# Values split one group ahead in attention, and slot lists read behind w2's low parts

## The chip, the cores and the metric

The program runs on one core of a Trainium2 chip. Its engines are TensorE (PE, with its weight loads shown as PEld), VectorE (DVE), ScalarE (ACT), GpSimd (POOL) and SyncE (SP, which here only issues transfers). The metric is the device time of one execution in microseconds (us); smaller is better.

## The reference

Causal attention for 4 batches of 12 heads, 448 rows of 64 values each, and behind it a mixture of 8 experts in which every token goes to one expert:

```python
scores = scale * np.matmul(q, k.transpose(0, 1, 3, 2))        # (4, 12, 448, 448), masked above the diagonal
attn = np.exp(scores - max) / (sum + 1e-09)
x = np.matmul(attn, v)  ->  (1792, 768)
logits = x @ w_gate + modality_bias[modality_id]
e_idx = np.argmax(logits, axis=1);  gate_w = softmax(logits) at e_idx
out[mask_e] = gate_w[mask_e, None] * (np.maximum(x[mask_e] @ w1[e], 0.0) @ w2[e])   # for each expert e
```

Everything is float32. w1 is 768 x 1024 and w2 is 1024 x 768 for each expert.

## The kernel before

The program is written as one fixed order of instructions for each engine; nothing is rescheduled. An engine stops at an instruction whose inputs or whose buffer are not ready, and all that stands behind it on that engine waits too. Float32 accuracy is had by splitting each number into a high and a low part (names with h and l) and adding products of the parts.

**Attention.** There are 48 heads (4 batches of 12), taken in 12 groups of `GH` = 4 heads. `iteration(n)` runs 48 times and is a pipeline over heads. In iteration n, PE makes the scores of head n (`st_scores`, L277), transposes the weights of head n-2 (`st_trans`, L306 and L313), multiplies the weights of head n-3 with the values (`st_pv`, L338 and L345), and for finished groups combines heads into token rows (`st_comb`, L398). ACT takes exponentials (L294), DVE the row maxima (L284) and low parts (L325), and both empty the products (L363, L369).

POOL feeds this in order. At odd n `split_qk((n + 3) // 2)` splits q and k of two heads (L185, L186, L189), which PE needs from iteration n+3 on; between, SP copies the parts into the stacked tile `st` (`stack_qk`, L197 and L198, at even n). At n % 4 == 1, `split_vh` and `split_vl` (L252, L257) split the values of group n // 4 from `vraw` into the tile `vhl`, which has two buffers. Group a's tile is first read by `st_pv` of head 4a in iteration 4a+3 and last by head 4a+3 in iteration 4a+6. `load_v` (L245, L246) has SP fetch the values of a group into the only `vraw`, at n = 4a, once the split of the group before has read it. POOL also normalises half of the token rows (`st_norm`, L416 and L426, at odd n), and for each of the four batches it scatters four slot lists into DRAM (`scatter`, L509). Near the end it splits w1 (L681, L682).

**Between attention and experts.** The first step of the experts (t = 0) has two blocks of 128 tokens, 0 and 1; all of this is straight code. PE runs the first product of both blocks (`pre_g1`), transposes h (`h_trans`, L793), and runs the second product `g2` (L765 to L767) with w2. w2 is split in 8 pieces, k = 0 to 7: `w2_chunk` has ACT make the high part (L684) and DVE the low part (L685). `g2` of block 0 needs piece k for its step k. For the step t = 1 SP reads the slot lists back (`ids_for(1)`, tile `idq`, L734), and `fetch_x(1)` has DVE merge the four lists into two index tiles (L744, L745, tile `idg`) and POOL gather the tokens' rows into `xg` (L746). `schedule_b` (L641 to L646, DVE), `schedule_c` (L651, one PE product) and `schedule_d` (L658 to L669, DVE) work out which expert comes in which step. `next_x(1)` has PE transpose `xg` (`x_trans`, L755); step 1 begins with `g1_pair`.

Of the kernel before, what the change touches and what calls it, by code (L numbers as in the profile page):

```python
# [21 lines left out]
def attention_moe(  # L22
# [15 lines left out]
    B, HP, _, _, S = qk.shape  # L38
# [6 lines left out]
    K2 = DF // 128  # L45
    GH = 4
    NG = H // GH
# [194 lines left out]
    def load_v(gr):  # L242
        b, u = divmod(gr, NG)
        c = slice(u * GH * D, (u + 1) * GH * D)
        nc.sync.dma_start(out=vraw[:, 0:3, :], in_=v[b, 0:384, c].rearrange("(t p) c -> p t c", p=128))  # L245
        nc.sync.dma_start(out=vraw[0:64, 3, :], in_=v[b, 384:448, c])  # L246
# [3 lines left out]
    def split_vh(gr):  # L250
        t = T([128, NTL, GH, 2, D], F32R, "vhl", 2)
        P.tensor_scalar(out=t[:, :, :, 0], in0=vsrc, scalar1=1.0, scalar2=0.0, op0=ALU.mult, op1=ALU.add)  # L252
        vhl[gr] = t

    def split_vl(gr):
        t = vhl[gr]
        P.tensor_tensor(out=t[:, :, :, 1], in0=vsrc, in1=t[:, :, :, 0].bitcast(F32), op=ALU.subtract)  # L257
# [127 lines left out]
    def st_comb(gr, i, x=None):  # L385
        b, u = divmod(gr, NG)
        q0, n = QT[i]
        if u == 0:
            xrow[b, i] = row()
            if i == 0:  # L390
                lt_all[b] = lts[b % 2]
                P.tensor_scalar(
                    out=lts[b % 2][:, :, H, :], in0=mb[:, b], scalar1=1.0, scalar2=0.0, op0=ALU.mult, op1=ALU.add
                )
        if x is None:
            x = bank("x")
        for j in range(GH // 2):
            nc.tensor.matmul(  # L398
                x[:n, j * 2 * XW:(j + 1) * 2 * XW], lhsT=ots(gr, j)[:, q0:q0 + n],
                rhs=wi[:, u * (GH // 2) + j].rearrange("p a c -> p (a c)"), start=True, stop=True,  # L400
            )
        cx[gr, i] = V, x
# [401 lines left out]
    def of_block(u):  # L804
        return lambda k: (2 * u + k // 4, (k % 4) * BLK)
# [85 lines left out]
    with tc.manual_schedule():  # L891
# [186 lines left out]
        def iteration(n):  # L1078
            if n and n % 2 == 0 and n + 2 < NHEAD:
                stack_qk((n + 2) // 2)  # L1080
            if n and n % GH == 0 and n < NHEAD:
                load_v(n // GH)
            gr, i = divmod(n - 2 * GH, GH)
            comb = 0 <= gr < B * NG
            if 0 <= n - 4 < NHEAD:
                st_out(n - 4)
            if comb:
                st_move(gr, i)
                st_norm(gr, i)
                b, u = divmod(gr, NG)  # L1090
                if u == NG - 1:
                    later(n + 1, lambda i=i: x_store(b, i))
                    if i == NTL - 1:
                        after_batch(b, n)
            run_todo((n,))
            if n in (2, 3):
                st_trans(n - 2)
            if n < NHEAD:
                st_scores(n)
            if n == 0:  # L1100
                subs.extend(first_split(1))
            if n in (1, 2):
                for f in subs[:1] if n == 1 else subs[1:]:
                    f()
            run_todo(n)
            if n == 0:
                split_vh(0)
                split_vl(0)
            if n in (1, 3):
                clear_kz(n // 2)  # L1110
            if n % 2 == 1 and n + 3 < NHEAD:
                split_qk((n + 3) // 2)
            if n % GH == 1 and n > GH:
                st_sums(n // GH - 1, P)
            if n % GH == RECAT and n > GH:
                st_rec(n // GH - 1)
            if n % GH == 1 and n > 1:
                split_vh(n // GH)
                split_vl(n // GH)
            if 0 <= n - 1 < NHEAD:  # L1120
                st_exp(n - 1)
            if 0 <= n - 2 < NHEAD:
                if n > 3:
                    st_trans(n - 2)
                run_todo(-n)
                st_split(n - 2)
            if 0 <= n - 3 < NHEAD:
                st_pv(n - 3)
                st_low(n - 3)
            gr, i = divmod(n - 2 * GH + 1, GH)  # L1130
            if 0 <= gr < B * NG:
                st_comb(gr, i)
            if n % 2 == 0 and n + 6 < NHEAD:
                load_qk((n + 6) // 2)

# [34 lines left out]
        def part2(t, b, at, late, mid, ys):  # L1170
            g2(ys, at, range(2))
            late()
            mid()
            g2(ys, at, range(2, K2))
            y_out(t, b, ys)
# [60 lines left out]
        def w2_chunk(*ks):  # L1236
            split_w(raw20, w2h, w2l, ks)
# [34 lines left out]
        pre_g1(1, (5,))  # L1272
        h_trans(0, hb, 1, pb)
        ids_for(1)
        fetch_x(1)
        ids_for(2)
        w2_chunk(4, 5)
        ys = [bank("ot"), bank("x")]
# [2 lines left out]
        ha, hb = (relu(o, i) for i, o in enumerate(g1b[1]))  # L1281
        h_trans(1, ha, 0, pa)
        w2_chunk(6, 7)
        sd = schedule_b(*sc_)
        g2(ys, of_block(0), range(4, K2))
        y_out(0, 0, ys)
# [9 lines left out]
                prefetch(0, raw2, w2, K2)  # L1296
                new_w1(1)

        part2(0, 1, of_block(1), lambda: None, mid1, two_banks())
        total = reg(sch[0:1, 4:5], mybir.ALL_ENGINES, 1, NSTEP)  # L1300

        def step(t):
# [121 lines left out]
```

## Time and profile before

| | |
|---|---|
| median of three runs | 534.66 us (532.64 to 536.38) |
| the profiled execution | 537.39 us, span of its instructions 535.7 us |
| attention, first scores to last product with values | 6.6 to 230 us of the span |
| attention to experts, straight code | 230 to 277 us |
| steps of the experts | 277 to 535.7 us |
| PE busy over the span | 484.6 us, 90% |

The three runs spread by 0.7%. A stretch of the span is named below by its start and end in us. In a timeline, the bracket at a row's end is how long the engine stood idle ahead of that instruction and what released it. PEclk is the clock that TensorE was granted, as a share of 2.4 GHz: 1.00 is 2.4 GHz and 0.50 is 1.2 GHz; a number between means that both occurred.

### The profile page before, as it was taken

Reading aid. Unit: us, or ns where it says so; the run is one execution under the profiler, and the core shown is the slowest. Engines: PE = TensorE matmul, PEld = TensorE weight load, DVE = VectorE, ACT = ScalarE, POOL = GpSimd, SP = SyncE. Lnnn points to the kernel's source line nnn. Section 1 sums busy time; section 2 is a strip of 40 time slices with the busy share of each in tenths; the row PEclk is TensorE's granted clock in tenths of the full one; section 3 lists DMA queues with packets and bytes.
Section 4 is the critical chain, followed back from the end, with each engine's and each line's share of the span. In section 5 each row is a group of like instructions: output and inputs, shape, how many; then the busy total and the mean of one; then the engine's idle time right before and its main releaser. Section 6 shows DMA issues by size and latency. Waiting matters only on the chain. (4 is left out here: it accounts for less than half of the span.)

```text
span 535.7 us, 10328 instructions
## 1 busy us (share of the span) xinstructions
PE 484.6 (90%) x3331; PEld 452.3 (84%) x3331; DVE 318.3 (59%) x882; ACT 274.0 (51%) x683; POOL 290.1 (54%) x303
## 2 busy tenths in 40 slices
PE   4789999999888979889799999999999999989971
PEld 4678889989777879778699999999999999978751
DVE  6899889999788999688341103652011120394690
ACT  4587889989687778434221213442112111452820
POOL 7997989889987797972120200841101001193581
PEclk9799999999899999899799999999999999999987
DMA  8697599986888489656259400784201001087000
GB/s 207 159 247 179 146 228 271 257 214 182 229 203 210 107 227 287 211 154 98 61 144 397 141 32 1 251 268 118 78 1 51 29 2 65 26 262 266 5 12 6
DMA packets 44137, 80.75 MB, mean 151 GB/s; under 512 B 15646, under 2 KB 27166, under 8 KB 44064
## 3 DMA queue, kind: packets, MB, share of 16 engines
q1 hardware_dynamic: 41024, 68.89, 47.5%
q0 software_dynamic: 3040, 11.03, 6.1%
q8 instruction: 28, 0.46, 0.4%
q14 instruction: 45, 0.37, 0.3%
HBM read 49.01 MB, written 11.89 MB: 114 GB/s over the span
## 5 line engine op out<-in xcount | busy, mean ns | idle before, releaser
L294 ACT ACTIVATE p<-p,nm 128x448 f32<-128x448 f32 x192 | 94.8, 497 | 3.9 <-DVE nm L284 3.9
L746 POOL DMA_INDIRECT xg<-xs,idg x18 | 20.3, 1129 | 136.1 <-DVEq L1334 75.2
L784 DVE SCALAR_TENSOR_TENSOR htl<-g,hth 128x256 fp32r<-128x256 f32 x40 | 16.8, 424 | 109.5 <-ACT hth L783 109.5
L767 PE MATMUL g<-xh,w1l 128*128 128x256 f32 x240 | 67.9, 283 | 0.0
L766 PE MATMUL g<-xl,w1h 128*128 128x256 f32 x240 | 67.9, 283 | 0.0
L765 PE MATMUL g<-xh,w1h 128*128 128x256 f32 x240 | 67.9, 283 | 0.0
L338 PE MATMUL ot<-ph,vhl 128*128 128x448 f32 x192 | 50.8, 305 | 16.0 <-POOL vhl L257 9.5
L306 PE MATMUL pt<-ident,p 128*128 128x128 f32 x432 | 65.2, 279 | 0.0
L325 DVE TENSOR_TENSOR pl<-pt,ph 128x1024 fp32r<-128x1024 f32 x48 | 58.3, 1216 | 10.8 <-ACT ph L324 10.5
L189 POOL TENSOR_TENSOR kz<-raw,hl 64x448 fp32r<-64x448 f32 x44 | 51.6, 1172 | 6.3 <-DMA table<-ent,si 2.6
L324 ACT ACTIVATE ph<-pt 128x1024 fp32r<-128x1024 f32 x48 | 48.9, 1020 | 11.1 <-PE pt L306 10.8
L306 PEld LDWEIGHTS pt<-ident,p 128*128 128x128 f32 x432 | 54.0, 151 | 0.7 <-issue 0.3
L338 PEld LDWEIGHTS ot<-ph,vhl 128*128 128x128 f32 x192 | 33.6, 194 | 19.2 <-POOL vhl L257 10.9
L783 ACT ACTIVATE hth<-g 128x256 fp32r<-128x256 f32 x40 | 15.2, 383 | 65.5 <-PE g L767 64.7
L825 POOL DMA_INDIRECT out_dram<-row,idg x14 | 14.8, 1056 | 58.5 <-ACTq L1318 32.2
L766 PEld LDWEIGHTS g<-xl,w1h 128*128 128x128 f32 x240 | 46.1, 192 | 0.0
L767 PEld LDWEIGHTS g<-xh,w1l 128*128 128x128 f32 x240 | 46.1, 192 | 0.0
L765 PEld LDWEIGHTS g<-xh,w1h 128*128 128x128 f32 x240 | 46.1, 192 | 0.0
L277 PE MATMUL sa<-st 128*128 128x448 f32 x96 | 32.6, 340 | 10.8 <-DVE st L229 8.3
L363 ACT ACTIVATE hol<-ot 64x448 f32<-64x448 f32 x48 | 26.0, 542 | 28.0 <-PE ot L338 27.2
L284 DVE CUSTOM_DVE_ANT_0 p<-sa,mask 128x448 f32<-128x448 f32 x96 | 36.3, 413 | 3.2 <-PE sa L277 1.3
L284 DVE CUSTOM_DVE_ANT_0 p<-sb,mask 128x192 f32<-128x192 f32 x96 | 36.3, 412 | 0.3
(337 smaller groups left out, 1408.1 us busy)
## 6 DMA issues: line engine op xcount, KB each, us to landing
st<-hl SPq DMA_DIRECT2D x88, 224.0 KB
raw<-in_moe_w_dram SPq DMA_DIRECT2D x24, 512.0 KB
raw<-in_qk_dram SPq DMA_DIRECT2D x22, 448.0 KB
raw<-in_moe_w_dram SPq DMA_DIRECT2D x20, 384.0 KB
vraw<-in_v_dram SPq DMA_DIRECT2D x12, 384.0 KB
xs<-row SPq DMA_DIRECT2D x12, 384.0 KB
ut<-in_moe_w_dram SPq DMA_DIRECT2D x6, 384.0 KB
raw<-in_qk_dram SPq DMA_DIRECT2D x8, 224.0 KB
```

The costliest lines, as they stand in the source:

```text
L189: P.tensor_tensor(out=kz[m % 2][r, a], in0=x[r, 1], in1=hl[r, 2].bitcast(F32), op=ALU.subtract)
L277: nc.tensor.matmul(outs[i], lhsT=a[:, q0:q0 + n], rhs=z[:, :w], start=(last == 0), stop=(last == 1))
L284: V.tensor_tensor_reduce(out=z, in0=o, in1=m, scale=-scale, scalar=3.0e38, op0=ALU.add, op1=ALU.min, accum_out=nm[:n, i:i + 1],)
L294: A.activation(out=z, in_=z, func=AF.Exp, bias=nm[:n, i:i + 1], scale=-1.0, accum_out=sums[:n, b, i, h:h + 1],)
L306: nc.tensor.transpose(out=o, in_=a, identity=ident)
L324: A.activation(out=ph, in_=t, func=AF.Copy)
L325: V.tensor_tensor(out=pl, in0=t, in1=ph.bitcast(F32), op=ALU.subtract)
L338: nc.tensor.matmul(o[:, q0:S], lhsT=t[:rows, kt, h].rearrange("p a d -> p (a d)"), rhs=ph[:rows, c0:c1], start=(n == 0), stop=(n == 1),)
L363: A.activation(out=t, in_=ov[g][64:128, :S], func=AF.Copy)
L765: nc.tensor.matmul(o, lhsT=ah, rhs=bh, start=first, stop=False)
L766: nc.tensor.matmul(o, lhsT=ah, rhs=bl, start=False, stop=False)
L767: nc.tensor.matmul(o, lhsT=al, rhs=bh, start=False, stop=last)
```

## The change

There are two edits.

The first moves the values one group ahead. `load_v(n // 4 + 1)` now stands at n % 4 == 0 (for group 1 in iteration 0, right behind the split of group 0), and `split_vh` and `split_vl` of group n // 4 + 1 stand at the end of the iterations with n % 4 == 2. The second moves `fetch_x(1)` behind the last two pieces of w2, and `mid1` (with `next_x(1)` and the gather for step 2) from behind two steps of block 1's `g2` to behind five.

```diff
         def iteration(n):
...
-            if n and n % GH == 0 and n < NHEAD:
-                load_v(n // GH)
+            if n and n % GH == 0 and n // GH + 1 < B * NG:
+                load_v(n // GH + 1)
...
             if n == 0:
                 split_vh(0)
                 split_vl(0)
+                load_v(1)
...
-            if n % GH == 1 and n > 1:
-                split_vh(n // GH)
-                split_vl(n // GH)
...
             if 0 <= gr < B * NG:
                 st_comb(gr, i)
+            if n % GH == 2 and n // GH + 1 < B * NG:
+                split_vh(n // GH + 1)
+                split_vl(n // GH + 1)
...
         ids_for(1)
-        fetch_x(1)
         ids_for(2)
...
         w2_chunk(6, 7)
+        fetch_x(1)
         sd = schedule_b(*sc_)
...
-        part2(0, 1, of_block(1), lambda: None, mid1, two_banks())
+        ys = two_banks()
+        g2(ys, of_block(1), range(5))
+        mid1()
+        g2(ys, of_block(1), range(5, K2))
+        y_out(0, 1, ys)
```

On POOL the instructions of the split stay almost where they were: the row `rec` ahead of them and the rows `ltp` and `row` behind are the same. This is POOL's order in iterations 29 to 31, where a scatter stands beside them (`vhl` is the split tile, `table` a slot list):

```order
 L189 TENSOR_TENSOR kz_149<-raw,hl 64x448 x2
 L376 TENSOR_SCALAR rec<-sums 128x16
-L252 TENSOR_SCALAR vhl<-vraw 128x16x64
-L257 TENSOR_TENSOR vhl<-vraw,vhl 128x16x64
 L509 DMA table_70<-ent,si 14592x2
+L252 TENSOR_SCALAR vhl<-vraw 128x16x64
+L257 TENSOR_TENSOR vhl<-vraw,vhl 128x16x64
 L416 TENSOR_TENSOR ltp<-cxt,rec 128x32
 L426 TENSOR_TENSOR row<-cxt,rec 128x256
```

The rows that moved now split the values of group 8 where they split those of group 7, and the scatter goes ahead of them. Their tile's buffer was last read by the head whose `st_pv` stands in the same iteration, so they wait for PE there; before, that read lay three iterations back.

At the start of SP's order, the load of group 1's values goes ahead of the load of q and k for heads 6 and 7 and of the first stacked copies (`st`), and it waits until POOL has split group 0:

```order
 L897 DMA bias_sb<-in_moe_modality_bias_dram 128x16
 L927 DMA wi<-in_moe_w_gate_dram 64x6x8 x2
+L245 DMA vraw<-in_v_dram 128x3x256
+L246 DMA vraw<-in_v_dram 64x256
 L179 DMA raw<-in_qk_dram 128x896
 L197 DMA st<-hl 64x896
```

The load at L179 and the four copies behind it moved back by two rows.

On DVE, between attention and experts, the merge of the slot lists (`idg`) stands behind w2's low parts (`w2l`) and the low part of h (`htl`):

```order
 L796 TENSOR_TENSOR htl_3378<-g,hth_3377 128x512
+L685 TENSOR_TENSOR w2l_3364<-raw_115,w2h_3363 128x768
+L685 TENSOR_TENSOR w2l_3366<-raw_116,w2h_3365 128x768
+L796 TENSOR_TENSOR htl_3380<-sa,hth_3379 128x512
+L685 TENSOR_TENSOR w2l_3368<-raw_3373,w2h_3367 128x768
+L685 TENSOR_TENSOR w2l_3370<-raw_3374,w2h_3369 128x768
 L744 TENSOR_REDUCE idg_0_119<-idq 128x1
 L745 TENSOR_REDUCE idg_0_119<-idq 128x1
 L744 TENSOR_REDUCE idg_1_120<-idq 128x1
 L745 TENSOR_REDUCE idg_1_120<-idq 128x1
-L685 TENSOR_TENSOR w2l_3364<-raw_115,w2h_3363 128x768
```

The five rows with a plus stood behind the merge before; the row with a minus is the first of them.

## Rows read from the trace of the kernel before

**Rows 1.** Stages: us; PE, PEld, DVE, ACT, POOL busy; PEclk; DMA share; GB/s

```profile
59.52:123.53 64.01, 62.21 (x504) 58.62 (x504) 59.10 (x193) 59.09 (x171) 57.40 (x64) 1.00 0.88 224
117.81:203.12 85.31, 75.34 (x575) 69.42 (x576) 76.04 (x244) 67.42 (x192) 72.81 (x77) 0.96 0.77 197
276.90:440.00 163.10, 163.10 (x1183) 162.93 (x1183) 40.35 (x84) 41.60 (x87) 30.02 (x23) 1.00 0.35 120
```

**Rows 2.** Who waited for whom on PE: total us, times, longest

```profile
PE ot L338 <- POOL vhl L257: 9.5, 7, 2.1
PE ot L338 <- DVE ut L369: 6.5, 6, 1.9
```

**Rows 3.** Timeline of PE in attention

```profile
189.54 0.44 PE L277 MATMUL sa<-st 128*128 128x448 f32 x1 [0.69 <-DMA st<-hl]
207.57 0.44 PE L277 MATMUL sa<-st 128*128 128x448 f32 x1 [0.31 <-DMA st<-hl]
216.07 0.56 PE L338 MATMUL ot<-ph,vhl 128*128 128x448 f32 x2 [1.61 <-POOL vhl L257]
```

**Rows 4.** Stretches in which PE's clock was down, columns as in Rows 1

```profile
139.03:142.13 3.10, 3.10 (x12) 2.28 (x12) 1.12 (x2) 1.04 (x3) 2.89 (x5) 0.53 0.73 270
158.72:164.00 5.28, 5.28 (x28) 4.45 (x29) 2.94 (x11) 2.51 (x9) 5.03 (x6) 0.68 0.53 119
216.07:221.00 4.93, 4.92 (x27) 4.40 (x28) 1.97 (x4) 2.51 (x9) 4.85 (x5) 0.67 0.24 71
259.85:265.45 5.60, 5.60 (x17) 5.60 (x18) 4.04 (x10) 0.00 (x0) 1.90 (x2) 0.50 0.51 141
```

**Rows 5.** Timeline of POOL in attention

```profile
86.02 1.05 POOL L252 TENSOR_SCALAR vhl<-vraw 128x1024 fp32r<-128x1024 f32 x1
87.15 2.39 POOL L257 TENSOR_TENSOR vhl<-vraw,vhl 128x1024 fp32r<-128x1024 f32 x1
92.41 2.41 POOL L189 TENSOR_TENSOR kz<-raw,hl 64x448 fp32r<-64x448 f32 x2
...
153.63 1.18 POOL L189 TENSOR_TENSOR kz<-raw,hl 64x448 fp32r<-64x448 f32 x1 [2.19 <-DMA table<-ent,si]
166.76 0.24 POOL L416 TENSOR_TENSOR ltp<-cxt,rec 128x32 f32<-128x32 f32 x1 [2.85 <-issue]
...
200.63 2.41 POOL L189 TENSOR_TENSOR kz<-raw,hl 64x448 fp32r<-64x448 f32 x2
```

**Rows 6.** The start: timelines of POOL, SP and PE

```profile
14.23 2.62 POOL L257 TENSOR_TENSOR vhl<-vraw,vhl 128x1024 fp32r<-128x1024 f32 x1
11.47 0.34 SPq L179 DMA_DIRECT2D raw<-in_qk_dram  x1
23.74 0.57 PE L277 MATMUL sa<-st 128*128 128x448 f32 x1
```

**Rows 7.** The start: two stages, columns as in Rows 1

```profile
17.00:18.00 1.00, 0.00 (x0) 0.00 (x0) 0.97 (x3) 1.00 (x6) 1.00 (x2) 1.00 0.00 0
21.00:26.00 5.00, 5.00 (x24) 4.78 (x23) 4.27 (x16) 2.02 (x8) 4.70 (x6) 0.50 0.96 252
```

**Rows 8.** Timelines of DVE, POOL, ACT and PE between attention and experts

```profile
258.57 0.16 DVE L744 TENSOR_REDUCE idg<-idq 128x1 int32<-128x4 int32 x1 [5.53 <-DMA idq<-table]
258.84 1.82 DVE L685 TENSOR_TENSOR w2l<-raw,w2h 128x768 fp32r<-128x768 f32 x2
261.03 1.03 POOL L746 DMA_INDIRECT xg<-xs,idg  x1 [0.30 <-issue]
256.68 1.56 ACT L684 ACTIVATE w2h<-raw 128x768 fp32r<-128x768 f32 x2
259.85 0.69 PE L766 MATMUL ot<-w2l,hth 128*128 128x384 f32 x1 [3.52 <-DVE w2l L685]
269.34 0.82 PE L755 MATMUL g<-ident,xg 128*128 128x128 f32 x6
```

**Rows 9.** Just after the gathered rows moved: one stage, columns as in Rows 1

```profile
265.00:266.00 1.00, 1.00 (x6) 1.00 (x5) 0.00 (x0) 0.00 (x0) 0.00 (x0) 0.74 0.02 6
```

## The prediction

> **What bounds the kernel now.** I read the stages first, then who waits on PE, then PE's and POOL's timelines around the longest waits. The stages [rows 1] show three regimes. From 276.9 to 440 us PE is busy all the time; whatever starts this stretch earlier ends the program earlier, one for one, since nothing there waits for anything but PE. In the middle of attention (59.52 to 123.53) PE is idle 64.01 - 62.21 = 1.8 us out of 64, and the four others are busy 57 to 59 us: five engines are within 10% of each other, so freeing one gives little. From 117.81 to 203.12 PE is busy only 75.34 of 85.31 us, and POOL 72.81.
>
> The edits aim at two waits. PE waits 9.5 us in seven places for the split of the values [rows 2]; the six waits for `ut` are DVE's and stay. Three of the seven are followed by a stretch at a lower clock [rows 4]: 3.10 us at 0.53 lose 3.10 x 0.47 = 1.5 us against the full clock, 5.28 us at 0.68 lose 1.7, 4.93 us at 0.67 lose 1.6, together 4.8. The other wait lies between attention and experts: DVE stands 5.53 us for the slot lists, w2's low parts are queued behind that, and PE waits 3.52 us for them [rows 8]. The 5.60 us that follow run at half the clock [rows 4], which loses 2.8.
>
> **The first edit: what goes.** If no wait for the values came in place of another, 9.5 + 4.8 = 14.3 us would go. That is the ceiling, for three reasons.
>
> The work on POOL is the same. Each group still costs it 1.05 + 2.39 us for the split [rows 5], in nearly the same place; only PE's need for the result comes four iterations later. So POOL's pace decides as soon as it is slower than PE's. That this happens is seen already: PE waits 0.69 us at 189.54 and 0.31 us at 207.57 for the stacked q and k [rows 3], which come from POOL's `split_qk` through SP. The second of these is the scores of head 46; POOL's work for it ended at 200.63 + 2.41 = 203.04 [rows 5]. Up to there PE cannot come out earlier than POOL does. POOL is idle 85.31 - 72.81 = 12.5 us between 117.81 and 203.12, but most of this is its own: twice 2.19 us and once 0.43 it waits for a scatter to land (one is in rows 5), and each scatter has gaps of some tenths around it. What goes when PE runs earlier is the wait of 2.85 us at 166.76 [rows 5], for a row that PE made late since it had stood and then run slowly from 158.72 on [rows 4]. With a smaller one of this kind I count 3.3 us for this stretch; the bounds are 2 (DVE, busy 76.04 us there, takes the rest) and 6 (POOL's idle time beyond its landings, half of it).
>
> The last wait for the values, 1.61 us at 216.07 [rows 3], and the 1.6 us of low clock behind it go in full. After head 46 PE needs nothing more from `split_qk`, and POOL no longer has a split there: it comes to the w1 pieces earlier than before. Bounds: 1.6 (the clock falls for another reason) and 3.2; I take 3.2.
>
> In the ordinary groups up to 123 us PE has 1.8 us of idle time and 0.9 more ahead of it; I take 2.0 (0.5 to 2.7).
>
> **The first edit: what it adds.** The start gets slower. SP may fetch group 1's values only when POOL has read group 0's, at 14.23 + 2.62 = 16.85 [rows 6]. Behind this in SP's order stand the load of q and k for heads 6 and 7, issued at 11.47 before [rows 6], and the copies for head 4. Values (448 x 256 numbers, 448 KB) and q, k (128 x 896, 448 KB) thus move between some 18.5 us and the copies. The DMA engines are empty at 17 to 18 us and move 252 GB/s at 21 to 26 us [rows 7]: 0.9 MB take 3.6 us, some 2 of which fit ahead of the copies. The scores of head 4, at 23.74 [rows 6], come some 2.0 us later, with 0 to 3.6 as bounds, and I see nothing that gives it back, for PE's next waits there are for DVE.
>
> The Trainium skill, page "DMA: Bandwidth & Descriptors", section "Queues, rings and completion order", speaks against this part: within SP's row of rings each DMA engine takes descriptors in the order in which they were put, so what is queued first goes first. By that the copies wait for all 0.9 MB and the start loses 3.6 us less the empty time, so no other sum; if they shared the engines instead, it could be 0. No run here shows which.
>
> The new wait is POOL's for PE: the split of group a+1 needs the buffer that head 4a-1 reads in the same iteration. Queued behind it on POOL are a normalisation and `split_qk` for head 4a+6. From the end of that product PE has three iterations, some 12 us, to head 4a+6 (16 iterations take 64.01 us [rows 1]). POOL needs 3.5 us for the split and 94.82 - 89.54 = 5.3 us from its end to the end of the next `split_qk` [rows 5], in all 8.8, and the copy must land. That leaves 3.2 us for the copy. I cost this wait at nothing; the cover is those 3.2 us. For head 46 the copy came 207.57 - 203.04 = 4.5 us after POOL's end, beside other transfers, so the cover can be gone.
>
> Sum for attention: -2.0 (start) + 2.0 + 3.3 + 3.2 = 6.5 us.
>
> **The second edit.** DVE makes w2's low parts without standing for the lists: the wait of 3.52 us and the 2.8 us of half clock go, 6.3. Two things come late next. ACT makes the high parts of pieces 6 and 7 from 256.68 to 258.24, and DVE's two low parts (1.82 us [rows 8]) end near 259.3; PE, now without a stop, wants the first of them at some 258.2 and waits 0.3. `schedule_b` then stands behind the merge (the lists were there at 258.57), which makes PE wait some 0.4 in `schedule_c`. So 5.6 us, with bounds 2 and 6.3.
>
> The gather's price is nothing as long as it lands before PE's transposes. It was issued up to 262.06 [rows 8] and its bytes had moved by 265.0, when the engines fall idle [rows 9], 3 us later. DVE merges some 0.7 us later than before, so it lands at 265.7. PE comes to the transposes at 269.34 - 5.6 plus three steps of `g2`. A matmul takes 5.60 / 17 = 0.33 us at half clock [rows 4], 0.165 at full, and a step has six: three steps are 3.0 us. That is 266.7, so 1.0 us is left; without the three steps PE would wait.
>
> **The sum.** 6.5 + 5.6 = 12.1 us. The profiled execution took 537.39 us and would take 525.3; it is 2.7 us over the median of the runs. Taken from the median, 534.66 - 12.1 = 522.6 us.
>
> **The rivals.**
> 1. *POOL takes the place of the waits.* Copies for q and k land as late as the values did, and of attention's gain only the last wait of 1.6 remains, the ordinary groups paying for the start. For it: both waits for copies in rows 3. Against it: only 1.0 us of them in the whole trace. 534.66 - 1.6 - 5.6 = 527.5.
> 2. *POOL has more room than counted.* All of 14.3 goes, less the start: 534.66 - 12.3 - 5.6 = 516.8. Against it: POOL's 72.81 us [rows 1].
> 3. *The slot lists come later against PE than before.* A scatter or a fetch slips by some us beside other transfers, PE stands in `schedule_c` or at the transposes, and the second edit brings 2 us: 526.2. For it: only 1.0 us is left for the gather.
> 4. *Slower: POOL waits for PE and then PE for POOL, in every group.* If the copy takes 4.5 us after POOL's end, as for head 46, and not under 3.2, PE waits 1.3 us at head 4a+6 in each of 10 groups, and the clock falls behind it (1.6 us each): 29 us. 534.66 + 29 - 14.3 - 5.6 = 543.8. Against it: in the ordinary groups no wait for a copy is seen.
>
> **How the numbers follow.** Forecast 0.60, rival 1 0.16, rival 2 0.09, rival 3 0.10, rival 4 0.05. The likeliest gives 522.6. Its own bounds are: start 0 to -3.6, ordinary groups 0.5 to 2.7, middle 2 to 6, last wait 1.6 to 3.2, second edit 2 to 6.3. They will not all fall on one side; half of the distance to each end gives some 516 to 528. Rivals 1 and 3 lie within 528; I set 515.5 to 529, which leaves rival 4 and a part of the others outside. A change of 1% is about what a measurement of this kernel can tell from none. Under 529.3 us lie the forecast, rival 2 and most of 1 and 3: 0.85; within 1%: 0.10; slower: 0.05.
>
> **What the profile after would show.** PE has no wait for `vhl` after the first groups. PE's waits for `st` grow beyond 1.0 us, and they stand where scatters are (160 to 205 us). POOL's 2.85 us ahead of a normalisation are gone, and a wait for PE stands ahead of the split. The scores of head 4 come near 25.7, those of head 46 some 3 us before 207.57. Behind the lists there is no stretch at half clock, and `g1_pair` starts some 12 us earlier than at 276.9. I am wrong if waits for `st` or `kz` with a low clock behind them stand in each group, if PE stands at its transposes of the gathered rows, or if the start loses over 4 us.

## The result and the profile after

The changed kernel took 529.11 us (median of 4 runs, 527.26 to 530.47) beside 534.97 us for the kernel before on the same chip: a ratio of 0.9892, 95% interval 0.9844 to 0.9941. Timed again on another chip (after_again, below) it took 527.46 against 530.94 us: 0.9940, 0.9913 to 0.9966. So it is faster, by 3 to 6 us where 12.1 were forecast, and 529.11 lies just above the range of 515.5 to 529.0. The profiled execution of before that the prediction was made from, 537.39 us, was one of its long ones; a second profile of before (before_again) was of a short one, 530.61 us, on a chip where the others took 530.63 to 537.89 us.

The profiled execution of the changed kernel took 529.8 us, its span 528.1. First who waits on PE (total us, times, longest), the rows of attention over 1 us, to be read against [rows 2]:

```profile
PE sa L277 <- DVE st L229: 8.5, 2, 6.7
PE ot L338 <- DVE ut L369: 5.0, 6, 2.1
PE sa L277 <- DMA st<-hl: 4.8, 5, 2.2
PE sa L277 <- DVE row L426: 2.9, 1, 2.9
PE sa L277 <- DVE kz L232: 2.0, 2, 1.0
PE x L484 <- DVE oh L474: 2.0, 2, 1.4
PE sa L277 <- DVE ut L369: 1.6, 1, 1.6
PE sa L277 <- DVE pl L325: 1.1, 1, 1.1
```

No wait for `vhl` is left. In its place stand waits of the scores (`sa`, line 277): 4.8 us for the copies of q and k, and 2.9, 1.6 and 1.1 us put down to DVE instructions that have nothing to do with the scores. In the second profile of the same kernel the waits at the same heads 14, 36 and 42 (0.72, 2.37 and 1.58 us) stand under the copies, so I read these rows as the copies too: 10.4 us of waits for copies (2.2 of them at head 4; before had 1.0 in all) came where 9.5 us of waits for values went. The two rows of `st` and `kz` from DVE are the first heads, as before. PE's timeline at the places that [rows 3] showed, and where the pair stage begins:

```profile
26.02 0.71 PE L277 MATMUL sa<-st 128*128 128x448 f32 x1 [2.23 <-DMA st<-hl]
66.97 0.44 PE L277 MATMUL sa<-st 128*128 128x448 f32 x1 [1.11 <-DVE pl L325]
158.86 0.56 PE L277 MATMUL sa<-st 128*128 128x448 f32 x1 [2.92 <-DVE row L426]
188.89 0.44 PE L277 MATMUL sa<-st 128*128 128x448 f32 x1 [1.64 <-DVE ut L369]
215.26 0.18 PE L484 MATMUL x<-oh,upper 128*128 128x32 bf16 x1 [1.41 <-DVE oh L474]
251.98 0.60 PE L793 MATMUL sa<-ident,hol 128*128 128x128 f32 x4
267.45 0.28 PE L765 MATMUL g<-xh,w1h 128*128 128x256 f32 x1
```

The stages (columns as in [rows 1]): heads 12 to 28, the middle of attention up to head 45, the low-clock stretch behind the last wait, and the stretch that ran at half clock:

```profile
58.19:123.39 65.20, 62.22 (x505) 58.62 (x504) 60.13 (x194) 59.38 (x171) 59.30 (x68) 1.00 0.88 224
117.60:202.00 84.40, 75.34 (x578) 70.36 (x578) 75.59 (x240) 67.63 (x193) 71.12 (x76) 0.96 0.80 197
215.39:218.99 3.60, 3.60 (x35) 3.18 (x32) 3.60 (x14) 3.40 (x11) 3.52 (x3) 1.00 0.95 320
255.00:262.00 7.00, 7.00 (x41) 6.69 (x42) 4.78 (x24) 1.70 (x3) 3.10 (x3) 1.00 0.46 108
```

Up to head 45 the middle takes 84.40 us where it took 85.31, at head 46 the changed kernel is 0.44 us ahead (207.13 against 207.57 in [rows 3]), and the ordinary groups take longer. Only the last two rows are what was forecast: no low clock, and PE busy all the time where it had stood 3.52 us.

Where heads' scores start, and what comes after attention, in all three profiles without the first edit and three with it (us; "lists" is the time from the hidden tile's transposes, 251.98 above, to the pair stage, 267.45 above):

| profile | head 4 | 9 | 31 | 36 | 42 | 47 | lists | span |
|---|---|---|---|---|---|---|---|---|
| before | 23.74 | 46.74 | 134.64 | 161.17 | 189.54 | 211.45 | 21.36 | 535.7 |
| before_again | 22.43 | 43.93 | 132.25 | 159.60 | 187.53 | 209.03 | 19.44 | 528.8 |
| second_alone | 23.37 | 46.33 | 134.22 | 160.05 | 188.30 | 212.57 | 15.48 | 528.1 |
| after | 26.02 | 46.76 | 134.49 | 158.86 | 188.89 | 210.81 | 15.47 | 528.1 |
| after_again | 25.45 | 45.97 | 134.23 | 158.25 | 187.03 | 209.42 | 15.48 | 526.5 |
| first_alone | 26.09 | 47.51 | 134.72 | 159.16 | 189.82 | 211.69 | 17.11 | 528.9 |

Head 47 starts at 211.0 us on the mean without the first edit and at 210.6 with it, while two profiles of before differ by 2.4 us there: no gain is seen. The last product with the values starts at 229.13, 224.74 and 227.22 us without the edit and at 226.84, 227.08 and 229.31 with it, which is no gain either. PE's next wait is ahead of the positions of the last batch (line 480), which come 10.5 to 10.6 us after that product without the edit and 9.1 to 9.2 us with it: this 1.4 us is the one gain of the first edit that all six profiles show. The lists' stretch takes 15.5 us with the second edit, each time, and 17.1 to 21.4 without it.

### The profile page after: what moved, and what is told of

The parts are those of the page before. It is cut to its first block, busy times and chain, and to the rows that moved or that the text cites. A ratio compares the mean times of both kernels' runs of the same rounds, so it can differ in the third digit from the quotient of the medians.

```text
span 528.1 us, 10324 instructions
## 1 busy us (share of the span) xinstructions
PE 480.4 (91%) x3331; PEld 449.1 (85%) x3331; DVE 316.4 (60%) x882; ACT 273.9 (52%) x683; POOL 289.3 (55%) x303
## 5 line engine op out<-in xcount | busy, mean ns | idle before, releaser
L325 DVE TENSOR_TENSOR pl<-pt,ph 128x1024 fp32r<-128x1024 f32 x48 | 58.3, 1214 | 12.3 <-ACT ph L324 12.1
L277 PEld LDWEIGHTS sa<-st 128*128 128x128 f32 x96 | 16.5, 171 | 24.4 <-DVE ut L369 7.6
```

The costliest lines, as they stand in the source:

```text
L277: nc.tensor.matmul(outs[i], lhsT=a[:, q0:q0 + n], rhs=z[:, :w], start=(last == 0), stop=(last == 1))
L325: V.tensor_tensor(out=pl, in0=t, in1=ph.bitcast(F32), op=ALU.subtract)
```

## The experiments

**The two edits apart, and the place of the early load and split.** *second_alone* is before with only `fetch_x(1)` and `mid1` moved; *first_alone* is before with only the values loaded and split early. These two sets of lines are in the diff of the change. The other two kernels alter the changed one:

```diff
 # v_later
 (at the top of iteration(n), behind stack_qk; the call in iteration 0 goes)
+            if n == 2:
+                load_v(1)
 # split_behind
 (behind split_qk instead of at the end of iteration(n))
-            if n % GH == 2 and n // GH + 1 < B * NG:
+            if n % GH == 3 and n // GH + 1 < B * NG:
                 split_vh(n // GH + 1)
                 split_vl(n // GH + 1)
```

> The kernel before with only the second edit (the gather of block 1 behind w2's last low parts, the transposes behind five hidden tiles of block 1). Theory: most of the 5.9 us that the change gave is this edit, and it works without the first one: 4 to 7 us below the kernel before, with no half clock between 255 and 275 us. Rival (the attention part gave the most): at most 2 us.

> The kernel before with only the first edit (values loaded and split one group ahead). Theory: inside attention POOL and the copies of q and k are late instead of the split, so that head 47's scores come within 1 us of the kernel before's 210.8 to 211.5 us, and all that is left is the low clock behind the last wait, some 1.6 us: 0 to 2.5 us below the kernel before in all. Rival (the waits for the split were worth what the prediction said): 6 us below.

> The changed kernel with the second group's values loaded behind the copies of heads 4 and 5 (iteration 2) instead of in iteration 0. Theory: head 4's scores come back from 26.0 to some 23.7 us, but nothing of it is left at head 9, since two waits for the bank of the outputs (1.3 and 1.9 us in the kernel before) take it: within 1 us of the changed kernel, 528 to 530 us. Rival (the start costs what the prediction took off, 2 us): 527 us or less, with every head from 4 to 47 about 2 us earlier.

> The changed kernel with the early split behind the second q, k split of a group (iteration 4g + 3) instead of ahead of it. Theory (the split that stands ahead of a pair's q, k split makes that pair's copies late): the waits ahead of heads 14 and 42 go, 1 to 2 us of the attention come back, 527 to 528 us. Rival (POOL's total work sets it, wherever the split stands, and other heads wait instead): 529 us as the changed kernel. Rival (the next pair is hit harder, having two iterations alone): 531 us.

Against 531.55 us for before on that chip: second_alone 529.26 us, 0.9945 (0.9918 to 0.9972), which is 1.5 to 4.4 us, between the rival's 2 at most and the 4 to 7 that I expected; first_alone 530.16 us, 0.9970 (0.9949 to 0.9991), 1.6 us, as expected, though its profile shows no gain up to the last product. v_later 531.28 us, 0.9992 (0.9963 to 1.0020), a miss: head 4 starts at 22.67 us, but the load, now queued ahead of the next pair's copies, makes head 6 wait:

```profile
35.89 0.71 PE L277 MATMUL sa<-st 128*128 128x448 f32 x1 [5.61 <-DMA st<-hl]
```

Head 31 starts at 138.79 us, 4.6 us after after_again's, and head 47 at 212.98. So the load costs whichever pair's copies stand behind it in SP's order. split_behind 535.09 us, 1.0065 (1.0038 to 1.0092): its second rival (531 us), and more. Who waits on PE there:

```profile
PE sa L277 <- DMA st<-hl: 17.5, 7, 4.2
PE ot L338 <- DVE ut L369: 2.9, 3, 2.0
```

These waits are ahead of heads 4, 8, 16, 24, 32, 36 and 44, that is nearly all ahead of the pair whose q, k split stands next behind the value split; ahead of heads 14 and 42, where the changed kernel waits, they are 0.2 us or none. The 3.4 us of split move with their place, and the copies behind them are late.

**Smaller steps of POOL and DVE.** All on top of the changed kernel: *after_again* is it unaltered; *split_shared* puts the low part behind the second q, k split and leaves the high part; *scatter_behind* issues the slot scatters behind `split_qk`, where the new `run_todo` stands; *choice_scalar* writes one comparison as four:

```diff
 # scatter_behind
-                later(n + 7 + (2 * i, i // 2, 0)[b], lambda i=i: scatter([i]))
+                later(n + (8.5 + 2 * i, 8.5, 7)[b], lambda i=i: scatter([i]))
+            run_todo(n + 0.5)
 # split_shared (behind split_qk; the call at the end of iteration(n) goes)
+            if n % GH == 3 and n // GH + 1 < B * NG:
+                split_vl(n // GH + 1)
 # choice_scalar
-            V.tensor_tensor(out=oh, in0=eq, in1=wide(m2), op=ALU.is_equal)
+            for t in range(NTL):
+                V.tensor_scalar(out=oh[:, t], in0=eq[:, t], scalar1=m2[:, t:t + 1], scalar2=None, op0=ALU.is_equal)
```

> The changed kernel unaltered, timed beside the three that follow on one chip: it is the line that they are held against. The two edits alone gave ratios of 0.9945 and 0.9970 to the kernel before; if they add up, 0.9915. If the first result stands, 0.989 or less (the edits help each other).

> The changed kernel with the slot scatters of batches 0 and 1 issued on POOL behind the q, k split of an odd iteration, so that each has a whole q, k period to land before the next second kz instruction, which waits for it. Theory (in the middle POOL and the copies behind it set the time): POOL's waits for a scatter's landing (6.9 us in three places) fall to under 2 us, the waits of 2.9 and 1.6 us ahead of the scores of heads 36 and 42 go, and 2 to 4 us come off: ratio to the changed kernel 0.993 to 0.996. Rival (the copies' own landing, on DMA queues that are full, sets it): POOL's waits go and the copies' stay, within 1 us of the changed kernel.

> The changed kernel with the routing's choice (one comparison of two tensors in SBUF, which took 1.81 us and ended with POOL's instruction beside it) written as four comparisons with a scalar per partition. Theory (a DVE instruction with two inputs in SBUF waits until POOL's is done): the four together take under 0.6 us also beside POOL's low part, PE's wait of 1.41 us ahead of the third batch's positions goes, and so do the 0.6 us at 105 us: 1 to 2 us less than the changed kernel. Rival (DVE is late for its own load there): PE waits 1 us or more all the same, no change.

> The changed kernel with the value split's high part (1.05 us) where the change put it and its low part (2.35 us) behind the second q, k split of the group: neither pair of q, k has the whole 3.4 us ahead of it. Theory (what is late is the pair whose split stands behind the value split, by as much as stands ahead of it): waits ahead of heads 14 and 42 shrink by two thirds, those ahead of heads 8, 16, 32, 44 grow by less than the 3.4 us that split_behind showed: 1 to 2 us below the changed kernel. Rival (the pair behind the low part has no room at all, as split_behind showed): 1 to 3 us above it.

Against 530.94 us: after_again 0.9940 (0.9913 to 0.9966), so nothing shows that the two edits help each other; scatter_behind 527.71 us, 0.9948 (0.9915 to 0.9982), and split_shared 528.19 us, 0.9952 (0.9923 to 0.9981), both the same as after_again, where both were expected to be faster. split_shared takes the wait ahead of head 14 away and gets 4.52 us ahead of head 44. In scatter_behind head 42 starts at 183.28 us, 3.8 us before after_again's, and then this follows:

```profile
198.96 0.71 PE L277 MATMUL sa<-st 128*128 128x448 f32 x1 [7.07 <-DMA st<-hl]
```

SP's read of the slot lists held the copies up there: it was issued at 185.41 us, the copies behind it from 194.23 on. POOL's waits for a scatter's landing, expected to fall under 2 us, are still 6.6 us there (6.9 in the changed kernel), so what POOL would gain without them stays untested. Neither order brings head 47 forward: it starts at 213.32 us in scatter_behind and at 215.16 in split_shared, after 209.42 in after_again. choice_scalar is slower, 534.16 us, 1.0057 (1.0025 to 1.0088), and shows why PE waited 1.41 us at 215.26. In the changed kernel, DVE's comparison in two places, and POOL's instruction beside the second:

```profile
153.41 0.19 DVE L473 TENSOR_TENSOR oh<-eq,m 128x32 bf16<-128x32 f32 x1
213.27 1.81 DVE L473 TENSOR_TENSOR oh<-eq,m 128x32 bf16<-128x32 f32 x1
212.65 2.39 POOL L682 TENSOR_TENSOR w1l<-raw,w1h 128x1024 fp32r<-128x1024 f32 x1
```

The same comparison takes 0.19 us or 1.81, and the long one ends at 215.08, POOL's low part at 215.04. In choice_scalar the first of the four runs from 214.46 to 216.22, POOL's low part to 216.19; together they end at 218.00, with POOL's next high part (217.97), and PE waits 3.13 us. So the four meet two POOL instructions, one after the other, and wait longer than the one. This agrees with the Trainium skill, page "SBUF — State Buffer", section "Who interferes with whom": a DVE instruction with two inputs in SBUF contends with a POOL instruction that reads SBUF, one in a two-port mode as well (it names `tensor_scalar` among those that can enter one), and there whoever comes second waits for the whole instruction. Whether the four ran in such a mode no run here shows. In the kernel before POOL stood idle there for the values, and the comparison met only the end of the short high part. The removed wait thus let POOL into DVE's way.

**A second profile of before, and two more orders.** *places_late* puts the positions of batches 0 and 2 and the rank steps one iteration later; *scatter_spread* is scatter_behind with other numbers; *places_scatter* is both.

```diff
 # places_late
+            o = b != 1
-            soon(n + 4, places)
+            soon(n + 4 + o, places)
-                (later if j % 2 else before)(n + 5 + j // 2, f)
+                (later if (j + o) % 2 else before)(n + 5 + (j + o) // 2, f)
 # scatter_spread
+                later(n + (8.5 + 2 * i, 6.5 + i // 2 * 2, 7)[b], lambda i=i: scatter([i]))
-                    later(n + 10 + t, lambda t=t: pre_ids(t))
+                    later(n + 11 + t, lambda t=t: pre_ids(t))
```

> The kernel before once more, for a second profile of it. Theory (the first profile of before, 537.4 us against a median of 531 to 535, had more wait in the routing tail than its usual execution, and the second edit's term was read from that): from the hidden tiles of the last batch to the pair stage (255.55 to 276.91 us, 21.4 us, in the first profile) some 17 us, as with the first edit alone (17.1), and the wait for w2's low part 1.6 us or less instead of 3.52. Rival (the wait is always there): 21 us.

> The changed kernel with the positions of batches 0 and 2 (PE's reader of the choice, and the rank steps behind it) one iteration later. Theory (DVE's comparison waits for POOL's instruction, and PE for the comparison): PE's waits of 0.8 us at 105 and 1.45 us at 214 go; the comparison itself stays as long, so that what DVE is late by comes back in part at the next scores: 0.5 to 2 us below the changed kernel. Rival (the DVE is what sets the pace there, whoever waits): no gain, 0 to 0.5 us.

> As scatter_behind, but with batch 1's scatters two behind the q, k split of iteration 37 and two behind that of 39, and the first slot lists read one iteration later, behind the copies of heads 44 and 45. Theory: the 7.07 us at head 44 in scatter_behind came from the list read, which held the copies up in SP's queue; without it head 44 starts at some 191 us (196.1 in the changed kernel's second profile), and 2 to 4 us come off. Rival (the scatters' landing, now behind the two splits of 39 and 41, or the lists' later landing, gives it back in the routing tail): no gain.

> Both of the last two edits on top of the changed kernel. If they are independent, their sum, 3 to 5 us below the changed kernel, 0.985 to 0.988 of the kernel before; if DVE and POOL are the bound whichever of them waits, no more than the better of the two.

before_again, 530.61 us, lies between theory and rival: 19.4 us, not 17 nor 21. Its two places, PE's rows and the stage behind the first:

```profile
213.28 0.56 PE L338 MATMUL ot<-ph,vhl 128*128 128x448 f32 x2 [1.21 <-POOL vhl L257]
255.40 0.44 PE L766 MATMUL ot<-w2l,hth 128*128 128x384 f32 x1 [2.60 <-DVE w2l L685]
213.28:218.00 4.72, 4.72 (x38) 4.27 (x39) 3.39 (x7) 2.57 (x10) 4.64 (x5) 1.00 0.23 70
```

The wait for w2's low part is 2.60 us, in first_alone 1.59, against 3.52 in [rows 8]. The last wait for the values is 1.21 us, and the clock behind it does not fall, where [rows 4] had 0.67. In after_again it does fall at that place, behind the wait for the comparison:

```profile
214.11:219.00 4.89, 4.89 (x32) 4.07 (x30) 3.72 (x13) 3.75 (x12) 4.81 (x4) 0.65 0.94 322
```

Against 534.91 us: places_late 533.83 us, 0.9982 (0.9950 to 1.0013); scatter_spread 531.32 us, 0.9943 (0.9914 to 0.9973); places_scatter 534.35 us, 0.9974 (0.9944 to 1.0003). In places_late the wait at 105 us goes, but head 26 starts at 114.38 us, after_again's at 114.46: the rival. At the end of attention the positions wait instead, 3.88 us, behind the row (line 426) that DVE normalises out of their bank. In scatter_spread a scatter issued at 185.06 lets POOL's second `kz` start only at 193.67, after a wait of 3.49 us, and head 44 still waits 4.62 us and starts at 198.82 us where 191 was expected. None of the three has a lower ratio than the changed kernel's 0.9892 and 0.9940, so places_late and scatter_spread ended with their rivals, and the two edits together are no better than the better of them.

**Which resource sets the pace.** *short_low_split* makes the low part for one of four token blocks (POOL), *no_v_load* leaves the later value loads out (DMA), *short_pl* makes the low part of the probabilities for 256 of 1024 columns (DVE), *short_low_pl* is the first and third:

```diff
 # short_low_split (vhl as two fixed tiles)
+        z = slice(0, NTL if gr < 2 else 1)
+        P.tensor_tensor(out=t[:, z, :, 1], in0=vsrc[:, z], in1=t[:, z, :, 0].bitcast(F32), op=ALU.subtract)
 # no_v_load
-            if n and n % GH == 0 and n // GH + 1 < B * NG:
+            if n and n % GH == 0 and n // GH + 1 < 2:
 # short_pl (pl as three fixed tiles)
+        z = slice(0, 1024 if g < 3 else 256)
+        V.tensor_tensor(out=pl[:, z], in0=t[:, z], in1=ph[:, z].bitcast(F32), op=ALU.subtract)
```

> The changed kernel with the value split's low part, from the third group on, made for one of its four blocks of tokens only (the other three keep the low parts of an earlier group), so that POOL's 2.35 us become some 0.6 us, 1.75 us in each of ten groups. Theory (POOL's order of work is what is late once the wait for the split is gone): the copies of q and k come earlier, PE's waits for them (9 us after head 8 in the changed kernel's second profile) go for the most part, head 47's scores come at 200 to 203 us instead of 209.4, and the run is 6 to 9 us shorter than the changed kernel, 0.977 to 0.983 of the kernel before. Rival (the copies' landing on full DMA queues): 207 us or later, no more than 2 us.

> The changed kernel without the load of the values from the third group on: POOL splits the second group's again (448 KB less per group on the DMA queues; the attention's output and so the routing differ, so that only the attention part, to head 47's scores, is to be compared). Theory (POOL): head 47's scores no more than 2 us earlier than 209.4 us. Rival (the DMA queues are the bound): 5 us or more earlier, and the waits for the copies gone.

> The changed kernel with the low part of the probabilities, from the fourth head on, made for 256 of 1024 columns only (the others keep those of an earlier head), so that DVE's 1.21 us become some 0.35 us in each of 45 heads. Theory (POOL): PE's waits for DVE (the output's bank, the choice; some 6 us after head 8) go, those for the copies stay or grow: head 47's scores 2 to 4 us earlier. Rival (DVE is the bound of attention): 8 us or more earlier.

> Both cuts, POOL's and DVE's. If PE waits for the one or the other in turn, more than either alone, head 47's scores at 198 to 201 us; if one of the two is the bound by itself, no more than that one alone.

| | POOL less | DMA less | DVE less | POOL and DVE less |
|---|---|---|---|---|
| median us (before: 529.62) | 516.73 | 526.11 | 525.14 | 515.13 |
| ratio | 0.9742 | 0.9944 | 0.9896 | 0.9724 |
| interval | 0.9707 to 0.9778 | 0.9905 to 0.9983 | 0.9853 to 0.9939 | 0.9696 to 0.9752 |
| head 47 at (after_again 209.42) | 201.43 | 208.33 | 209.30 | 198.84 |
| last batch's positions at (after_again 236.22) | 225.89 | 233.60 | 233.67 | 222.66 |

POOL it is. Its low part takes 0.73 us instead of 2.39 in ten groups, 16.6 us less, and head 47 comes 8.0 us earlier. 448 KB less per group on the DMA queues bring 1.1 us. DVE's low part takes 0.42 us instead of 1.21 for 45 heads, 36 us less, and brings 0.1 where 2 to 4 were expected, and 2.6 once POOL has room, as expected if PE waits for the one or the other in turn. At the last positions less on POOL brings 10.3 us, and less on DMA or DVE 2.6 each; the two profiles of before differ by 4.4 us there, so only the first is clear. The stage from 42 to 117 us in after_again, then with less on POOL, then with less on DVE:

```profile
42.00:117.00 75.00, 72.05 (x584) 67.93 (x584) 69.04 (x222) 68.40 (x199) 68.78 (x86) 1.00 0.90 225
```
```profile
42.00:117.00 75.00, 74.25 (x604) 70.10 (x603) 71.19 (x237) 71.30 (x204) 62.23 (x86) 1.00 0.91 232
```
```profile
42.00:117.00 75.00, 72.63 (x592) 69.01 (x591) 58.92 (x231) 69.70 (x202) 69.01 (x87) 1.00 0.88 225
```

PE is busy 74.25 of 75 us when POOL has 6.5 us less to do, and 72.6 when DVE has 10 us less; POOL's own busy time is the same then (69.01 and 68.78 us). In short_low_split PE's waits for copies after head 4 are one of 0.34 us, and DMA share and bytes are higher than in after_again. That one is ahead of head 36. SP's issue of the copy that waits for POOL's low part, and the scores that wait for it, in after_again and then with less on POOL:

```profile
151.01 0.62 SPq L198 DMA_DIRECT2D st<-hl  x1
158.25 0.44 PE L277 MATMUL sa<-st 128*128 128x448 f32 x1 [2.37 <-DMA st<-hl]
```
```profile
145.90 0.62 SPq L199 DMA_DIRECT2D st<-hl  x1
153.19 0.44 PE L279 MATMUL sa<-st 128*128 128x448 f32 x1 [0.34 <-DMA st<-hl]
```

From the issue to the scores it is 7.2 and 7.3 us, but the issue comes 5.1 us earlier: the copies land in time because POOL hands them over in time, not because they move faster. In no_v_load PE does not wait at head 36, and then 5.10 us ahead of head 42, whose low part POOL ends at 181.27 us, 0.6 earlier than in after_again:

```profile
185.93 0.71 PE L277 MATMUL sa<-st 128*128 128x448 f32 x1 [5.10 <-DMA st<-hl]
```

**Moving POOL's work instead of leaving it out.** *high_on_act* is the changed kernel with the high parts of the value split on ACT; *late_high_on_act* is second_alone with the same:

```diff
-        P.tensor_scalar(out=t[:, :, :, 0], in0=vsrc, scalar1=1.0, scalar2=0.0, op0=ALU.mult, op1=ALU.add)
+        A.activation(out=t[:, :, :, 0], in_=vsrc, func=AF.Copy)      # from the second group on
```

> The changed kernel with the high part of every value split but the first made on ACT, which is busy 69 of 75 us and 76 of 93 us in the two stretches of attention, instead of on POOL: 1.05 us less on POOL in each of eleven groups, about as much more on ACT. Nothing is left out. Theory (POOL sets the pace of attention; 17.5 us taken from it gave 8.0 at head 47): some 5 us earlier at head 47 (204 to 206 us), 3 to 5 us below the changed kernel, 0.984 to 0.988 of the kernel before. Rival (ACT becomes the one that PE waits for, through the exponentials): no gain or a loss, waits of PE for p or ph.

> The same with the values loaded and split where the kernel before has them (second_alone with the high parts on ACT): whether the first edit is worth its waits once POOL has room. Theory: the wait for the split's low part shrinks by the 1.05 us that POOL does not do, but is still there; the kernel lies between second_alone (0.9945) and high_on_act, 2 us or more above the latter. Rival (the first edit is worth nothing, with room or without): both the same within 1 us.

Against 530.35 us: high_on_act 527.58 us, 0.9947 (0.9923 to 0.9972), no better than the changed kernel, as the rival said. Its stage:

```profile
42.00:117.00 75.00, 71.40 (x570) 66.51 (x570) 68.68 (x219) 71.76 (x203) 62.56 (x79) 1.00 0.82 209
```

POOL has as little to do as in short_low_split (62.56 against 62.23 us), but ACT is busy 71.76 of 75 us, and PE 71.40. The waits of PE for `p` or `ph` that the rival named are not there; PE waits 6.8 us in 11 places for `ut` (4.7 in 8 in after_again). That ACT's load is the reason is therefore argued, not shown. late_high_on_act takes 569.89 us, 1.0745 (1.0701 to 1.0789); both of its theories are wrong. ACT stands for the load there, with the exponentials queued behind, and PE then stands for those:

```profile
73.78 1.06 ACT L253 ACTIVATE vhl<-vraw 128x1024 fp32r<-128x1024 f32 x1 [5.43 <-DMA vraw<-in_v_dram]
```
```profile
75.54 0.69 PE L309 MATMUL pt<-ident,p 128*128 128x128 f32 x2 [3.07 <-ACT p L297]
```

So the first edit is worth 42 us where ACT makes the high parts, and almost nothing where POOL does. No kernel tried, of those that compute everything, beats the changed one by more than its interval.

## Why the prediction was wrong

I compare the profiles of before and after, from which the forecast and the result come, and call before_again and after_again the second pair.

**The start: size right, permanence different from pair to pair.** Head 4 came 2.28 us later (2.0 forecast, "nothing that gives it back"), in the second pair 3.02. At head 9 the difference is 0.02 us: two waits for `ut`, 1.29 and 1.92 us in before, became 0.78 us. before_again does not have these two waits, and in the second pair 2.04 us of the start are still lost at head 9.

**Ordinary groups: -2.0 + 2.0 forecast, 0.14 us measured** at head 28 (123.39 against 123.53), and -1.98 in the second pair (123.12 against 121.14). Where the sum is right, its parts are not: the start was given back before head 9, the vhl waits (1.92 us) went, and new waits of 1.11 us (head 14), 0.61 (head 16) and 0.63 us (for the choice, at 105 us) took their place.

**The middle: the step that failed.** 3.3 us were forecast, with 2 as the lower bound; between head 28 and head 46 the gain is 0.44 - 0.14 = 0.3 us. In the second pair it is 2.1 us, but that only makes good what the start had cost: head 46 starts at 205.18 us there, in before_again at 205.34. The prediction took its 3.3 us from POOL's idle time and said that PE cannot come to head 46 before POOL has made its part. That bound held, and 2.85 us of POOL's idle time did go, as forecast. What failed is that POOL would therefore be done earlier. In the changed kernel its last instruction for heads 46 and 47, against 200.63 in [rows 5], and its waits for a scatter's landing are:

```profile
201.22 2.41 POOL L189 TENSOR_TENSOR kz<-raw,hl 64x448 fp32r<-64x448 f32 x2
POOL kz L189 <- DMA table<-ent,si: 6.9, 3, 3.3
```

It ends at 203.63 us, and in after_again and first_alone at 202.32 and 204.61; in before, before_again and second_alone it ends at 203.04, 201.02 and 202.17. That is 1.4 us later on the mean with the first edit, where 3.3 us earlier was forecast. In the first pair the waits for landings grew from 4.8 us, which the prediction took as fixed, to 6.9; in the second pair they are 6.8 and 6.5, so their size is not the edit's doing, and what fills POOL's time differs from one execution to the next.

On PE the failure shows in the wait that the prediction costed at nothing, on a cover of 3.2 us for the copies behind the split. The heads whose q, k split stands next behind the value split waited 1.11 (head 14), 0.41 (34), 1.64 (42) and 0.32 us (46), together 3.5, and heads 8, 16, 32, 36 and 44, for which the prediction had no term, another 5.5: 9.0 us where before waits 1.0 us ahead of the same heads. POOL's timeline ahead of head 36, the longest of them:

```profile
147.29 1.00 POOL L509 DMA_INDIRECT table<-ent,si  x1 [0.50 <-issue]
...
151.27 1.17 POOL L189 TENSOR_TENSOR kz<-raw,hl 64x448 fp32r<-64x448 f32 x1
155.10 1.14 POOL L189 TENSOR_TENSOR kz<-raw,hl 64x448 fp32r<-64x448 f32 x1 [2.66 <-DMA table<-ent,si]
156.61 1.04 POOL L252 TENSOR_SCALAR vhl<-vraw 128x1024 fp32r<-128x1024 f32 x1
```

It stands 2.66 us for a scatter between the two halves of `kz`, which makes all that is behind it late. Head 36 itself does not wait for that: its copies were issued by 151.96 us. In after_again and short_low_split they took equally long (above), and what differs is when POOL handed them over. In the main this is rival 1 (527.5 us, 0.16): POOL takes the place of the waits. short_low_split shows it, split_behind shows that the lateness goes where the split goes. That after_again's 527.46 us is the rival's number is luck, since its 1.6 us of the last wait is not found in every pair and its 5.6 us of the second edit is too much. POOL's own wait for PE is small, as costed: 0.49, 0.52 and 0.75 us in three places, of which this is one:

```profile
86.39 1.05 POOL L252 TENSOR_SCALAR vhl<-vraw 128x1024 fp32r<-128x1024 f32 x1 [0.49 <-PE ot L338]
```

**The last wait: 3.2 us forecast, 1.65 measured** from head 47's scores to the last product's (226.84 against 229.13, less 0.64). The wait of 1.61 us was replaced by one of 1.41 for DVE's comparison, which POOL, free earlier, held up; what came is the low clock's 1.6. That clock is no property of the kernel: before_again has none there, after_again has it, and in the second pair this stretch takes 1.95 us longer with the edit (17.66 against 15.71 us).

**The second edit: 5.6 us forecast, 5.9 in this pair of profiles** (21.36 against 15.47), with no stop and no half clock, as described. But it was priced from the one execution with the longest wait. In other executions of kernels without the edit that stretch takes 19.44 and 17.11 us, 4.0 and 1.6 us more than with it, and timed alone the edit gives 2.9 us (1.5 to 4.4). Taking terms from an execution 2.7 us over the median, and then taking them in full from the median, was the second failure. A further 1.43 us came between the last product and the last batch's positions, unforeseen; 1.02 of it is PE's wait ahead of these, 1.39 us in before and 0.37 at 235.96 here. This belongs to the first edit: the wait is 1.39 to 1.79 us in the three profiles without it and 0.37 to 0.41 in the three with it.

**The end.** From 481.64 on, the first small tile, the changed kernel took 46.46 us, before 44.67: DVE stood 1.13 us for a list (below), and over the first 44 us the granted clock was 0.87 against 0.89. after_again takes 44.67 us, so this was that execution alone.

```profile
492.00 0.16 DVE L744 TENSOR_REDUCE idg<-idq 128x1 int32<-128x4 int32 x1 [1.13 <-SPq L1329]
```

The sum of the pair: 0.64 + 1.65 + 1.43 - 0.15 + 5.89 - 1.79 = 7.67 us; with 0.07 lost in the pair stages that is the spans' difference, 7.6. (The 0.15 lie between the positions and the transposes.) The 1.6 us that first_alone gained when timed may be the 1.4 us behind the last product, the only gain of the first edit that its profile shares with the other two; that is not shown, and why DVE has that row earlier was not followed up. Left open: why the start was given back in one pair and not in the other, and why the middle gained only in that other.

**The range.** Half of the distance to each end of the bounds gives 519.5 to 527.4 us, not the 516 to 528 that the prediction worked out.

## What to carry to other kernels

A wait that was taken away here came back at the next thing that the late engine makes, because that engine had no less to do: eight orders of the same work began head 47 at 209 to 220 us, none below the 209 to 213 of the kernels without the early split, and only leaving out POOL's work brought it below 208. When engines are busy within 10% of each other, ask by an experiment that leaves work out which of them sets the pace, and do it before planning an order; moving the work to an engine that was itself nine tenths busy returned nothing here. Price a wait from two profiles: here the same wait was 3.52, 2.60 and 1.59 us, and a low clock stood behind it or did not.

## What the runs showed of the hardware

A DVE comparison of 128x32 elements took 0.19 us while POOL stood idle and 1.81 us beside a POOL instruction, whose end it shared to 0.04 us; split into four of 128x8 it took 2.91 us in one place and 3.54 in another, each time up to the end of a second POOL instruction. An indirect scatter of 128 rows issued while the DMA engines were at work let the instruction that waits for it start 7.8 us (147.29 to 155.10) and 8.6 us (185.06 to 193.67) after its issue. In the same place of the same program the granted clock was 0.67 or 1.00 in before, 1.00 or 0.65 in the changed kernel, from one execution to the next.
